# A second pair of heads ahead of the weights, and a new order for the first steps of an attention and two MLPs

## The chip, the cores and the metric

One core of a Trainium2 chip. The time is the device time of one execution in microseconds (us), the median over several runs.

## What is computed

Attention over a causal window of 128 positions with a linear bias per head, then two MLPs one after the other. All of it is float32.

```python
scores = scale * np.matmul(q, k.transpose(0, 1, 3, 2))        # q, k, v: (4, 8, 576, 64)
mask = (rel >= 0) & (rel < 128)
scores = np.where(mask, scores + bias[None], -1000000000.0)
attn = softmax(scores)
x = np.matmul(attn, v) -> (2304, 512)
h = x @ w_in                                                  # (512, 2048)
g = np.where(h >= 1, h, np.where(h <= -1, 0.0, (h + 1) ** 2 / 4))
x = g @ w_out                                                 # (2048, 512)
h = x @ w_in2
out = (h * np.clip(h + 3.0, 0.0, 6.0) / 6.0) @ w_out2
```

The weights reach the chip as 64-bit floats and are turned into 32-bit ones there.

## The kernel before

The tokens are cut into twelve **units** of 64 to 256 tokens (three to a batch). A unit has eight heads, and a head one or two **steps** of up to 128 query rows; the first unit has 256 tokens, so 16 steps. `tick` (L601) makes one step of the attention go one stage further for several steps at once:

- `stage_a` (L414) of the newest step: PE multiplies queries by keys (the scores, L411), VectorE adds the bias table and takes the row's bound (L441, here called the row), ScalarE takes the exponential (L445).
- `stage_b` (L454), two ticks later: PE transposes the probabilities (L469, L470), ScalarE copies them to `tt` (L152).
- `stage_c_whole` (L491), three ticks later: PE multiplies by the values into `r` (L506); at the end of a pair of heads VectorE divides by the sum (L518 to L520).
- `stage_d_whole` (L525), four or five ticks later: PE transposes the result (L531), ScalarE and VectorE split it into the two halves of `x` (L152, L159), which the first MLP reads.

The lags stand in `LAG_B, LAG_C, LAG_D` (L34). In `tick` the older steps' stages come first and `stage_a` last. While the first unit runs, `keep_busy` (L121) puts one matmul of zeros before each step's scores; `WARM_UP` pairs of such matmuls stand at the very start (L851). The tile `zeros` that they read is cleared by VectorE (L846), and ScalarE copies one column of it (L849).

Pairs of heads are loaded by `load_whole` (L307) and `load_values` (L319): two key transfers, one query transfer, one value transfer, all issued by SyncE's queue (SP). A pair's key and query tiles and its value tile are used again by later pairs, so a load waits for the steps that read the tile before. SP works its list strictly in the order in which the code is written; eight transfers may be in flight, since the ninth waits for the first to land. The other engines' lists are put in order by a scheduler, which an edge can bind: `behind` (L630) puts what it encloses behind the newest row on VectorE.

A weight block f is two transfers of 512 KB, `w_in` and `w_out` (L182, L186), given out by `Weights.load` (L172). Its conversion goes in three parts. `conv1` (L189) is two passes of ScalarE (L194, L198) and one of GpSimd (L197); `conv2` (L200) is two of VectorE (L205, L212); `conv3` (L214) is a cast of ScalarE (L152) and a subtraction of VectorE (L159). `conv_tick` (L222) does conv2 and conv3 of one block and conv1 of the next. During the first unit it is called four times, in ticks that the loop at L860 picks out:

```python
for t in range(n_pre):                 # n_pre = 20
    att.tick()
    if t % 2 == 0:
        W1.load()
    if t in (n_pre // 2 - 1, n_pre - 6) or t >= n_pre - 2:
        W1.conv_tick()
```

Then the first MLP begins. `Mlp.first` (L648) makes `h` in twelve matmuls per block (L655), `activate` (L680) makes `g` on VectorE (L684, L686), ScalarE (L685, L152) and GpSimd (L159), and `Mlp1.second` (L691) multiplies by `w_out` into `acc` (L697), two blocks of f later. The attention of the later units and the remaining conversions run between these matmuls.

Of the kernel before, what the change touches and what calls it, by code (L numbers as in the profile page):

```python
# [9 lines left out]
F32 = mybir.dt.float32  # L10
# [5 lines left out]
AF = mybir.ActivationFunctionType  # L16
ALU = mybir.AluOpType

P = 128
# [3 lines left out]
EPS = 1e-09  # L23
# [10 lines left out]
LAG_B, LAG_C, LAG_D = 2, 3, 4  # L34
LAG_B_SPLIT, LAG_C_SPLIT = 3, 5
WARM_UP = 6
WHOLE = 4


@with_exitstack  # L40
def tile_window_attention_two_mlps(
# [15 lines left out]
    nc = tc.nc  # L57
    B, H, D, S = qT.shape
# [189 lines left out]
    for j, (t0, n) in enumerate(units):  # L248
        for h in range(H):
            u = Head()  # L250
# [19 lines left out]
    class Attention:  # L270
# [137 lines left out]
        def scores(self, u, ps, qo, ko, nk):  # L408
            parts = [(u.q, u.k)] if u.whole else [(u.qs, u.kh), (u.qs, u.kl)]
            for w, (q, k) in enumerate(parts):  # L410
                nc.tensor.matmul(ps[:, :nk], q[:, qo:qo + P], k[:, ko:ko + nk],  # L411
                                 start=(w == 0), stop=(w == len(parts) - 1))

        def stage_a(self, n, i):  # L414

            u = heads[n]
# [18 lines left out]
            if not u.whole and a >= P:  # L435
# [8 lines left out]
                scalar=3.0e38, op0=ALU.add, op1=ALU.min, accum_out=sm[:, 0:1])  # L444
            nc.scalar.activation(out=pt[:, :nk], in_=pt[:, :nk], func=AF.Exp, bias=sm[:, 0:1],  # L445
                                 scale=-1.0, accum_out=None if u.whole else sm[:, 1:2])
# [44 lines left out]
        def stage_c_whole(self, n, i):  # L491
# [18 lines left out]
            if j == 0 or i < len(u.qbs) - 1:  # L510
# [6 lines left out]
            rec, r, y = rec[:, :nb], r[:, :nb], y[:, :nb]  # L517
            nc.vector.tensor_scalar(out=rec, in0=r[:, :, 0:2 * D + 2:2 * D + 1], scalar1=EPS, scalar2=None, op0=ALU.add)  # L518
            nc.vector.reciprocal(rec, rec)
            nc.vector.tensor_tensor(  # L520
                out=y, in0=r[:, :, 1:2 * D + 1].rearrange("p b (h d) -> p b h d", h=2),
                in1=rec.rearrange("p b (h o) -> p b h o", o=1).to_broadcast([P, nb, 2, D]), op=ALU.mult)
            u.y = y
# [77 lines left out]
        def tick(self):  # L601
            t = self.t
            self.t += 1
            first, whole = unit_steps[0], sum(unit_steps[:WHOLE])
            for lag, span, stage in ((LAG_D, range(first), self.stage_d_whole),
                                     (LAG_D + 1, range(first, whole), self.stage_d_whole),
                                     (LAG_C, range(whole), self.stage_c_whole),
                                     (LAG_C_SPLIT, range(whole, len(steps)), self.stage_c),
                                     (LAG_B, range(whole), self.stage_b),
                                     (LAG_B_SPLIT, range(whole, len(steps)), self.stage_b)):  # L610
                if t - lag in span:
                    stage(*steps[t - lag])
            if t < len(steps):
                n, i = steps[t]
                u = heads[n]
                self.more_loads(n + 3)
                self.more_preps(n)
                self.stage_a(n, i)
                late, self.late = self.late, []
# [6 lines left out]
            else:  # L626
                while self.late:
                    self.to_x(*self.late.pop(0))

        def behind(self):  # L630
# [206 lines left out]
    with ExitStack() as actx:  # L837
# [10 lines left out]

        nc.scalar.copy(zeros[:, 0:1], nc.const_aps.tensor(0.0, [P, 1], F32))  # L849
        bank = psum.tile([P, BANK], F32, tag="h1", name="busy")  # L850
# [3 lines left out]
        for vt in att.vts:  # L854
            nc.gpsimd.memset(vt[:, :, 0:2 * D + 2:2 * D + 1], 1.0)
        att.more_loads(1)
        W1.load()

        n_pre = unit_steps[0] + LAG_D
        for t in range(n_pre):  # L860
            att.tick()
            if t % 2 == 0:
                W1.load()
            if t in (n_pre // 2 - 1, n_pre - 6) or t >= n_pre - 2:
                W1.conv_tick()

# [469 lines left out]
```

## Time and profile before

| | us |
|---|---|
| median of 3 runs | 948.12 |
| lowest and highest run | 947.30, 948.22 |
| the profiled execution | 946.91 |
| its span, first to last instruction | 945.20 |
| PE busy in the span | 928.9 (98%) |
| VectorE, ScalarE, GpSimd busy | 659.8, 535.4, 306.1 |
| granted clock of TensorE, mean | 0.999 |

The profile is of one execution. Its engines are PE (matmuls; PEld is the loading of weights beside them), DVE (VectorE), ACT (ScalarE), POOL (GpSimd) and SP (SyncE, whose queue is SPq). An operation is named by its line, and out<-in by the tiles it writes and reads. Times in a timeline count from the start of the span.

### The profile page before, as it was taken

Reading aid. Unit: us, or ns where it says so; the run is one execution under the profiler, and the core shown is the slowest. Engines: PE = TensorE matmul, PEld = TensorE weight load, DVE = VectorE, ACT = ScalarE, POOL = GpSimd, SP = SyncE. Lnnn points to the kernel's source line nnn. Section 1 sums busy time; section 2 is a strip of 40 time slices with the busy share of each in tenths; the row PEclk is TensorE's granted clock in tenths of the full one; section 3 lists DMA queues with packets and bytes.
Section 4 is the critical chain, followed back from the end, with each engine's and each line's share of the span. In section 5 each row is a group of like instructions: output and inputs, shape, how many; then the busy total and the mean of one; then the engine's idle time right before and its main releaser. Section 6 shows DMA issues by size and latency. Waiting matters only on the chain.

```text
span 945.2 us, 17238 instructions
## 1 busy us (share of the span) xinstructions
PE 928.9 (98%) x5683; PEld 875.2 (93%) x5683; DVE 659.8 (70%) x1750; ACT 535.4 (57%) x1349; POOL 306.1 (32%) x575
## 2 busy tenths in 40 slices
PE   8899999999999999999999999999999999999998
PEld 6799999999999999999999999999999898888987
DVE  6998975786677677767647989848557777644443
ACT  6998854676667566666636876425333334423233
POOL 3243844787668676777710000000000000000000
PEclk9999999999999999999999999999999999999999
DMA  8858332232222212322007880004264644543441
GB/s 258 238 170 271 107 93 88 68 86 68 73 61 76 77 47 62 88 76 61 3 34 251 298 276 22 1 23 167 79 211 167 235 171 151 169 123 112 122 113 67
DMA packets 95337, 114.90 MB, mean 122 GB/s; under 512 B 8848, under 2 KB 73616, under 8 KB 95248
## 3 DMA queue, kind: packets, MB, share of 16 engines
q1 hardware_dynamic: 95248, 113.80, 38.2%
q8 instruction: 45, 0.74, 0.3%
q14 instruction: 44, 0.36, 0.1%
HBM read 88.60 MB, written 25.17 MB: 120 GB/s over the span
## 4 chain that ended last, share of the span: by engine, by line
PE 85%; DVE 6%; DMA 3%; ACT 3%; issue 1%; POOL 1%; SPq 0%; ACTq 0%; POOLq 0%; DVEq 0%
PE h L655 25%; PE acc L756 21%; PE acc L697 17%; PE y L1237 7%; PE x L1237 5%; PE s L411 3%; PE r L554 3%; DMA rawa<-w_out 2%; PE t L470 2%; PE r L506 1%; DMA rawa<-w_in 1%; DVE kl L391 1%; DVE r L684 1%; DVE r L686 1%; DMA qw<-qT 1%
## 5 line engine op out<-in xcount | busy, mean ns | idle before, releaser
L655 PE MATMUL h<-x,wa 128*128 128x384 f32 (+1 forms) x1344 | 231.0, 317 | 1.2 <-DVE r L686 0.8
L697 PE MATMUL acc<-g,wa 128*128 128x384 f32 (+1 forms) x1344 | 227.7, 315 | 0.4 <-POOL g L159 0.4
L756 PE MATMUL acc<-wb,g 128*128 128x512 f32 x861 | 222.2, 393 | 0.0
L655 PEld LDWEIGHTS h<-x,wa 128*128 128x128 f32 x1344 | 206.6, 189 | 4.3 <-DVE r L686 3.1
L697 PEld LDWEIGHTS acc<-g,wa 128*128 128x128 f32 x1344 | 206.2, 189 | 1.0 <-POOL g L159 0.6
L756 PEld LDWEIGHTS acc<-wb,g 128*128 128x128 f32 x861 | 159.4, 188 | 24.9
L152 ACT CAST g<-r 128x384 fp32r<-128x384 f32 (+1 forms) x208 | 101.3, 487 | 70.4 <-DVE r L1184 37.6
L159 POOL TENSOR_TENSOR g<-r,g 128x256 fp32r<-128x256 f32 (+1 forms) x96 | 93.4, 973 | 67.5 <-ACT g L152 51.4
L685 ACT ACTIVATE r<-r 128x384 f32<-128x384 f32 (+1 forms) x112 | 53.5, 478 | 80.4 <-DVE r L684 79.8
L159 DVE TENSOR_TENSOR g<-r,g 128x384 fp32r<-128x384 f32 x112 | 62.4, 557 | 43.2 <-ACT g L152 42.8
L684 DVE TENSOR_SCALAR r<-h 128x384 f32<-128x384 f32 (+1 forms) x112 | 55.4, 495 | 45.0 <-PE h L655 38.2
L488 POOL TENSOR_SCALAR_AFFINE_SELECT tt<-dist 128x256 fp32r<-128x256 f32 (+1 forms) x176 | 76.5, 455 | 14.0 <-DVE dist L483 13.9
L686 DVE TENSOR_TENSOR r<-h,r 128x384 f32<-128x384 f32 (+1 forms) x112 | 55.8, 499 | 27.9 <-ACT r L685 26.1
L655 PE MATMUL h<-x,wb 128*128 128x384 f32 x384 | 72.5, 336 | 0.0
L655 PEld LDWEIGHTS h<-x,wb 128*128 128x128 f32 x384 | 68.2, 188 | 2.6
L445 ACT ACTIVATE p<-p,sm 128x128 f32<-128x128 f32 (+2 forms) x134 | 57.0, 427 | 21.0 <-DVE sm L441 20.8
L1182 ACT ACTIVATE r<-u 128x384 f32<-128x384 f32 x32 | 16.8, 526 | 56.5 <-DVE u L1246 56.5
L554 PEld LDWEIGHTS r<-tt,vs 128*128 128x128 f32 x304 | 44.7, 189 | 3.1 <-issue 1.4
L393 POOL TENSOR_TENSOR qs<-qr,qs 128x256 fp32r<-128x256 f32 (+2 forms) x64 | 39.4, 616 | 25.1 <-ACT qs L390 13.3
L554 PE MATMUL r<-tt,vs 128*128 128x128 f32 (+3 forms) x304 | 44.3, 262 | 1.3 <-POOL tt L488 0.9
L470 PE MATMUL t<-ident,p 128*128 128x128 f32 x134 | 38.4, 288 | 1.0 <-DVE sm L448 0.5
L391 DVE SCALAR_TENSOR_TENSOR kl<-kr,kh 128x256 fp32r<-128x256 f32 (+3 forms) x64 | 38.9, 608 | 0.0
(161 smaller groups left out, 1553.6 us busy)
## 6 DMA issues: line engine op xcount, KB each, us to landing
w<-wd SPq DMA_DIRECT2D x88, 256.0 KB, 2.7
rawa<-w_in SPq DMA_DIRECT2D x16, 512.0 KB, 5.2
rawa<-w_out SPq DMA_DIRECT2D x16, 512.0 KB, 5.4
rawb<-w_in SPq DMA_DIRECT2D x16, 512.0 KB, 3.9
rawb<-w_out SPq DMA_DIRECT2D x16, 512.0 KB, 4.9
wd<-sum SPq DMA_DIRECT2D x32, 256.0 KB, 2.2
wd<-wb SPq DMA_DIRECT2D x24, 256.0 KB, 2.8
out<-o SPq DMA_DIRECT2D x17, 256.0 KB, 2.2
```

The source lines that it names most:

```text
L152: nc.scalar.copy(hi, x)
L159: engines[eng].tensor_tensor(out=lo, in0=x, in1=hi.bitcast(F32), op=ALU.subtract)
L445: nc.scalar.activation(out=pt[:, :nk], in_=pt[:, :nk], func=AF.Exp, bias=sm[:, 0:1], scale=-1.0, accum_out=None if u.whole else sm[:, 1:2])
L470: nc.tensor.transpose(ps[:, 1, :], pt[:, P:] if u.whole and has_prev else pt[:, :P], ident)
L488: nc.gpsimd.affine_select(out=u.tt[:, :, s0 + s, :m], in_=both, compare_op=ALU.is_ge, fill=0.0, base=-1 + s, pattern=[[0, 2], [sign, m]], ...
L554: nc.tensor.matmul(u.r[:, qo:qo + nq], u.vs[:, j, c, :, :].rearrange("p a d -> p (a d)"), u.tt[:, part].rearrange("p s q -> p (s q)")[:, s ...
L655: nc.tensor.matmul(ps[:, :n], self.W.w_in(a, c, f), self.x_chunk(x, b, c, n), start=(k == 0), stop=(k == 3 * KC - 1))
L684: nc.vector.tensor_scalar(out=r[:, :n], in0=ps[:, :n], scalar1=-1.0, scalar2=1.0, op0=ALU.max, op1=ALU.min)
L686: nc.vector.tensor_tensor(out=r[:, :n], in0=ps[:, :n], in1=r[:, :n], op=ALU.max)
L697: nc.tensor.matmul(acc[i][:, o * n:(o + 1) * n], self.W.w_out(a, f)[:, e * P:(e + 1) * P], g[:, b, :n], start=(first and k == 0 and o == 0 ...
L756: nc.tensor.matmul(acc[t][:, :DM], g[:, b, tg * P:(tg + 1) * P], self.W.w_out(a, f), start=(first and k == 0), stop=(last and k == 2))
L1237: nc.tensor.matmul(ps[:, :N2], w[:, a, c * P:(c + 1) * P], self.x.operand(k, c, b), start=(start and n == 0), stop=(n == 5), skip_group_ch ...
```

## The change

Four things are changed, all in the first unit of the attention:

- Before the loop two pairs of heads are loaded in place of one, and then two weight transfers in place of one; the loop's first tick no longer issues a weight transfer.
- In `tick`, a step of the first unit has its `stage_a` before the older steps' stages. In ticks 4 to 7 the stages c and d are bound behind the newest scores on PE, and the first unit's division is bound behind the newest row on VectorE.
- ScalarE's first copy writes `minus_odd`, which VectorE writes again later, in place of a column of `zeros`.
- The four conversion ticks are 8, 12, 16 and 19 in place of 9, 14, 18 and 19, and what they put on VectorE and ScalarE is bound behind the newest row and the newest exponential.

```diff
+CONV_AT = 8, 12, 16, 19
...
-                nc.tensor.matmul(ps[:, :nk], q[:, qo:qo + P], k[:, ko:ko + nk],
-                                 start=(w == 0), stop=(w == len(parts) - 1))
+                self.score = nc.tensor.matmul(ps[:, :nk], q[:, qo:qo + P], k[:, ko:ko + nk],
+                                              start=(w == 0), stop=(w == len(parts) - 1))
...
-            nc.scalar.activation(out=pt[:, :nk], in_=pt[:, :nk], func=AF.Exp, bias=sm[:, 0:1],
+            self.exp = nc.scalar.activation(out=pt[:, :nk], in_=pt[:, :nk], func=AF.Exp, bias=sm[:, 0:1],
...
+            with self.behind() if u.unit == 0 else ExitStack():
...
+            if t < first:
+                self.more_loads(steps[t][0] + 3)
+                self.more_preps(steps[t][0])
+                self.stage_a(*steps[t])
...
-                    stage(*steps[t - lag])
+                    with self.behind_score(t, lag):
+                        stage(*steps[t - lag])
...
-                self.more_loads(n + 3)
-                self.more_preps(n)
-                self.stage_a(n, i)
+                if t >= first:
+                    self.more_loads(n + 3)
+                    self.more_preps(n)
+                    self.stage_a(n, i)
...
+        def behind_score(self, t, lag):
+            second = range(4, 8)
+            return tc.issue_after(self.score.ins) if t in second and lag > LAG_B else ExitStack()
+
+        def behind_exp(self):
+            return tc.issue_after(self.exp.ins)
...
-        nc.scalar.copy(zeros[:, 0:1], nc.const_aps.tensor(0.0, [P, 1], F32))
+        nc.scalar.copy(minus_odd, nc.const_aps.tensor(0.0, [P, 1], F32))
...
-        att.more_loads(1)
+        att.more_loads(3)
+        W1.load()
         W1.load()
...
-            if t % 2 == 0:
+            if t % 2 == 0 and t > 0:
                 W1.load()
-            if t in (n_pre // 2 - 1, n_pre - 6) or t >= n_pre - 2:
-                W1.conv_tick()
+            if t in CONV_AT:
+                with att.behind(), att.behind_exp():
+                    W1.conv_tick()
```

SP's list, from its fifth transfer on; `kw`, `qw` and `vr` are keys, queries and values of a pair of heads, `rawa` a weight block. Before, then now:

```order
L182 DMA rawa_169<-w_in 128x4x256
L315 DMA kw_106<-kT 64x256
L317 DMA qw_107<-qT 128x256
L315 DMA kw_106<-kT 64x256
L327 DMA vr_103<-v 128x2x128
L186 DMA rawa_169<-w_out 128x1024
L315 DMA kw_kh_109<-kT 64x256
```

```order
L316 DMA kw_106<-kT 64x256
L318 DMA qw_107<-qT 128x256
L316 DMA kw_106<-kT 64x256
L328 DMA vr_103<-v 128x2x128
L183 DMA rawa_173<-w_in 128x4x256
L187 DMA rawa_173<-w_out 128x1024
L316 DMA kw_kh_109<-kT 64x256
```

The second pair's four transfers have moved up past `w_in`; from `w_out` on the list is as it was.

PE's list where the second pair's scores stand (`s` from `kw_106`); `t` are transposes of the probabilities, `r` products with the values of the first pair. Before, from the fourth step's scores on, then now:

```order
L506 MATMUL r_204<-vr_102,tt_188 128x65 x2
L470 MATMUL t_0_219<-ident,p_115 128x128
L469 MATMUL t_1_230<-ident,p_113 128x128
L470 MATMUL t_1_230<-ident,p_113 128x128
L506 MATMUL r_204<-vr_102,tt_218 128x65 x3
L411 MATMUL s_0_222<-kw_106,qw_107 128x128
L411 MATMUL s_1_234<-kw_106,qw_107 128x256
L411 MATMUL s_0_255<-kw_106,qw_107 128x128
```

```order
L412 MATMUL s_0_216<-kw_106,qw_107 128x128
L126 LDWEIGHTS zeros
L126 MATMUL s_1_229<-zeros 128x256
L507 MATMUL r_210<-vr_102,tt_198 128x65 x2
L471 MATMUL t_0_225<-ident,p_115 128x128
L412 MATMUL s_1_229<-kw_106,qw_107 128x256
L507 MATMUL r_210<-vr_102,tt_224 128x65
L470 MATMUL t_1_236<-ident,p_113 128x128
```

The second pair's first scores stood behind all products of the first pair; now they stand ahead of most of them.

VectorE's list where the first conversion step stands (L205 before, L206 now); the ISA instructions are the rows, `p_113` from `s_0_354` before and from `s_0_348` now the first of pair four. Before, then now:

```order
L441 ISA p_113,sm_1_301<-s_1_298,dist 128x256
L441 ISA sm_1_301 128x1
L518 TENSOR_SCALAR rec_310<-r_268 128x4
L205 SCALAR_TENSOR_TENSOR ma_304<-ma_304,rawa_169 128x1024
L519 RECIPROCAL rec_310<-rec_310 128x4
L441 ISA p_114,sm_0_326<-s_0_323,dist 128x128
```

```order
L442 ISA p_115,sm_1_334<-s_1_331,dist 128x256
L442 ISA sm_1_334 128x1
L521 RECIPROCAL rec_316<-rec_316 128x4
L522 TENSOR_TENSOR y_317<-r_274,rec_316 128x256
L442 ISA p_113,sm_0_351<-s_0_348,dist 128x128
L442 ISA sm_0_351 128x1
L206 SCALAR_TENSOR_TENSOR ma_293<-ma_293,rawa_173 128x1024
```

The step has moved back by three rows of the attention.

## Rows read from the trace of the kernel before

**Rows 1.** Busy time by stretch: length; each engine's us and instructions; granted clock; DMA share; GB/s.

```profile
0.00:5.00 5.00, 2.66 (x13) 1.91 (x14) 3.10 (x9) 1.48 (x2) 4.05 (x19) 1.00 0.34 93
5.00:10.00 5.00, 4.78 (x34) 3.79 (x33) 1.72 (x11) 2.80 (x8) 0.93 (x3) 1.00 0.96 296
10.00:15.00 5.00, 4.66 (x33) 3.52 (x32) 2.68 (x14) 3.60 (x10) 0.14 (x1) 1.00 1.04 308
15.00:20.00 5.00, 4.29 (x30) 3.17 (x30) 4.22 (x12) 4.25 (x11) 0.99 (x1) 1.00 1.05 301
20.00:40.00 20.00, 16.01 (x110) 13.46 (x109) 17.69 (x41) 18.43 (x33) 6.85 (x7) 1.00 1.01 291
40.00:60.00 20.00, 19.36 (x148) 18.11 (x148) 19.32 (x48) 18.83 (x40) 6.88 (x8) 1.00 0.38 118
60.00:945.20 885.20, 877.14 (x5327) 831.28 (x5326) 611.07 (x1618) 485.99 (x1249) 286.29 (x540) 1.00 0.36 115
```

The engines stand in the order PE, PEld, DVE, ACT, POOL.

**Rows 2.** Timeline from the start to the first row: start, us, instruction, idle before and releaser.

```profile
0.90 0.17 DVE L846 MEMSET zeros<- 128x128 uint32 x1 [0.90 <-PEq L1329]
...
2.34 2.74 PE L125 MATMUL busy<-zeros 128*128 128x256 bf16 x12 [2.34 <-ACT zeros L849]
...
4.88 0.42 PE L125 MATMUL s<-zeros 128*128 128x256 bf16 x1
...
5.15 0.15 DVE L130 TENSOR_SCALAR minus_odd<-odd 128x1 f32<-128x1 int32 x1
...
5.73 0.29 DVE L441 CUSTOM_DVE_ANT_0 p<-s,dist 128x128 f32<-128x128 f32 x1 [0.43 <-PE s L411]
```

**Rows 3.** Timeline of SP's queue: transfers of pair two, three and four.

```profile
3.79 0.52 SPq L315 DMA_DIRECT2D kw<-kT  x1
...
7.15 0.58 SPq L317 DMA_DIRECT2D qw<-qT  x1
...
11.60 0.35 SPq L317 DMA_DIRECT2D qw<-qT  x1
```

**Rows 4.** Timeline of ScalarE: pair two's exponentials, first conversion, cast of block three.

```profile
11.31 1.15 ACT L445 ACTIVATE p<-p,sm 128x128 f32<-128x128 f32 x3 [1.82 <-DVE sm L441]
...
13.62 1.15 ACT L194 ACTIVATE ma<-rawa 128x1024 f32<-128x1024 f32 x1
...
32.54 1.08 ACT L152 CAST wa<-ma 128x1024 fp32r<-128x1024 f32 x1
```

**Rows 5.** Landing of the query transfers issued at 7.15 and 11.60 us.

```profile
DMA to landing us min/median/max: 5.0/5.0/5.0
...
DMA to landing us min/median/max: 5.5/5.5/5.5
```

**Rows 6.** The transfers' queue in 2:4.5, 4.5:6.6, 6.6:30: packets, MB, mean rate or share.

```profile
DMA packets 553, 0.39 MB, mean 155 GB/s; under 512 B 57, under 2 KB 553, under 8 KB 553
...
q1 hardware_dynamic: 553, 0.39, 55.8%
...
q1 hardware_dynamic: 580, 0.56, 85.5%
...
DMA packets 6067, 7.06 MB, mean 302 GB/s; under 512 B 474, under 2 KB 5434, under 8 KB 6065
```

**Rows 7.** Timeline of PE: pair three's first scores, the first MLP matmul, second products.

```profile
13.73 0.39 PE L411 MATMUL s<-kw_kh,qw 128*128 128x128 f32 x2
...
23.10 0.98 PE L655 MATMUL h<-x,wa 128*128 128x256 f32 x6
...
40.74 0.74 PE L697 MATMUL acc<-g,wa 128*128 128x256 f32 x4 [0.39 <-POOL g L159]
```

**Rows 8.** Timeline of VectorE: first step of the first conversion, and its subtraction.

```profile
16.07 1.25 DVE L205 SCALAR_TENSOR_TENSOR ma<-ma,rawa 128x1024 uint32<-128x1024 uint32 x1
...
21.82 1.23 DVE L159 TENSOR_TENSOR wa<-ma,wa 128x1024 fp32r<-128x1024 f32 x1 [0.22 <-ACT p L445]
```

**Rows 9.** The page's groups: GpSimd's part of g.

```profile
L159 POOL TENSOR_TENSOR g<-r,g 128x256 fp32r<-128x256 f32 (+1 forms) x96 | 93.4, 973 | 67.5 <-ACT g L152 51.4
```

More of the change, by code (lines that the diff above doesn't have):

```diff
@@ L517, in stage_c_whole @@
             rec, r, y = rec[:, :nb], r[:, :nb], y[:, :nb]
[L518 to L522, printed above, removed]
+            with self.behind() if u.unit == 0 else ExitStack():
+                nc.vector.tensor_scalar(out=rec, in0=r[:, :, 0:2 * D + 2:2 * D + 1], scalar1=EPS, scalar2=None, op0=ALU.add)
+                nc.vector.reciprocal(rec, rec)
+                nc.vector.tensor_tensor(
+                    out=y, in0=r[:, :, 1:2 * D + 1].rearrange("p b (h d) -> p b h d", h=2),
+                    in1=rec.rearrange("p b (h o) -> p b h o", o=1).to_broadcast([P, nb, 2, D]), op=ALU.mult)
             u.y = y
```

## The prediction

> **What bounds the kernel now.** I read the table of stretches first, then the page's costliest groups, then the timeline of the first 41 us engine by engine, and last the DMA queue. The table [rows 1] shows TensorE (PE) busy for 877.14 of the 885.20 us after 60 us: from there it sets the pace, and nothing that the diff touches runs there. Before, it is not so. Between 5 and 40 us PE is idle for 0.22 + 0.34 + 0.71 + 3.99 = 5.26 us, between 40 and 60 us for 0.64 us. In the same stretches ScalarE (ACT) works 4.25 of 5 us and 18.43 of 20 us, VectorE (DVE) 4.22 of 5 and 17.69 of 20, and the DMA engines stand at a share of 1.0. So the ramp is where time can be won, it has three limits that lie close together, and the prize is no more than 5.26 + 0.64 us and what the first matmul can move.
>
> A microsecond saved in the ramp is worth a microsecond at the end if PE still has it when its waits are over. The printed order makes that simple to ask: behind the first ninth of PE's list, somewhere before 100 us, both kernels list the same instructions on every engine. The whole difference is how much earlier PE comes to that place.
>
> **The zeros.** Now PE's first weight load waits until 2.34 us for ACT's copy of one column of zeros; VectorE's own write of them ended at 0.90 + 0.17 = 1.07 us [rows 2]. With that copy aimed at another tile, PE starts 1.27 us earlier, and twelve warm-up matmuls and the first filler at (4.88 - 2.34)/12 = 0.21 us each are over at 3.8 us. The first scores follow there, and no longer at 5.1 us. The row behind them does not gain that much: VectorE is writing zeros into key tiles and two small constants until 5.30 us, in both kernels, so the first row moves from 5.73 to 5.30 us, **0.43 us**. The write of the constant now also waits for ACT's copy, which is over before 2.34 us and 2.8 us ahead of it; it costs nothing.
>
> **Pair two ahead of the weights.** SP gives out one transfer in 0.5 us [rows 3]. Four more of them in front of the first weight piece put that piece back by four issues, 2.1 us, and give PE the second pair's queries and keys before 7 us. Now ACT stands idle for 1.82 us before the exponentials of that pair at 11.31 [rows 4]. With the data there and the scores listed ahead of the lagging values, the idle goes, and ACT is through with both pairs near 12 us. It then has nothing, because pair three sits in the queue where it sat. Its queries land at 7.15 + 5.0 = 12.1 us now [rows 3, 5].
>
> They will land later. While only the attention's small transfers are in flight (2 to 4.5 us) the engines' share is 55.8%; in the 2.1 us after that, with the first weight piece among them, 85.5%; from 10 us on it is full, 1.04 and more [rows 1, 6]. In the new order the middle stretch looks like the first one. That loses (0.855 - 0.558) x 2.1 = 0.62 us of work, 0.6 us of every landing behind it while the engines stay full. The bounds: nothing, if the engines catch up because later pieces overlap better, and 1.0 us, if the stretch moves only the 155 GB/s of the first where it could move the 302 of the third: 2.1 x (1 - 155/302). I take 0.6, since it is nearest to what the stretch itself shows. The Trainium skill, "DMA: Bandwidth & Descriptors", section "Measured (HBM→SBUF, 128 partitions, SWDGE, issued from GpSimd)", speaks against this part: it gives 138 GB/s for transfers of 64 KB and 341 for 1 MB, which would make the lag 2.1 x (1 - 138/341) = 1.25 us, an estimate from that page, and the sum below 946.5 us in place of 945.9; the trace agrees in kind, 155 against 302 GB/s, and by less.
>
> So pair three's queries land near 12.7 us, its first exponential stands at 12.7 + 0.3 (second key tile) + 0.4 (scores, [rows 7]) = 13.4 to 13.5 us, and the first conversion behind it at **13.8 us** instead of 13.62 [rows 4]. By then one exponential and one copy more are done, 0.5 us. Net 0.3 us ahead: the idle is not removed, most of it moved from before pair two to before pair three.
>
> **Conversions queued.** This part takes something away. VectorE's first conversion step runs at 16.07 us now [rows 8]. In the new list it stands behind the first row of pair four, whose queries land at 11.60 + 5.5 = 17.1 us [rows 3, 5], 17.7 with the lag. Scores 0.4 and the row 0.3 us bring the step to 18.4 us, **2.3 us later**. Then 1.25, a row of 0.5, 1.25, ACT's cast of 1.08 and the subtraction of 1.23 [rows 4, 8]: the first MLP matmul can start at 23.7 us instead of 23.10 [rows 7], 0.6 us later. In exchange ACT's first conversion runs in one piece, and its second starts right behind pair four's first exponential, at 18.8 us.
>
> I follow ACT's list from there with the durations of these rows (each next instruction starts about 0.1 us before the end of the last). The cast of the first block ends at 22.5 us; then the remaining exponentials and copies of the unit and conversion three bring the second cast to 29.1, and the third begins at 33.8 us, 1.2 us later than the 32.54 of now [rows 4]. But ahead of it in the new list stand five instructions that stand behind it now: an exponential, a copy, a cast of x, one conversion step and a square, 0.4 + 0.3 + 0.3 + 1.07 + 0.3 = 2.3 us. ACT is ahead by 2.3 - 1.2 = **1.1 us**. VectorE, by the same count at its fourth subtraction, is ahead by 0.7 us. Both have 1.57 and 2.31 us of idle between 20 and 40 us now [rows 1], and my count allows for hardly any; that is its weak side.
>
> PE comes out better. The first g needs the third cast, two conversion steps and a cast, 34.7 + 2.1 + 0.3, and POOL's 0.97 us [rows 9]: second products can begin at 38.1 us instead of 40.74 [rows 7], 2.6 us earlier. Whether PE keeps that depends on ACT and DVE, which between 40 and 60 us work 18.83 and 19.32 of 20 us: PE would wait for them again until only their lead is left. I take the engine that I could follow best, ACT with 1.1 us, rounded down to **1.0 us** for the 0.7 of VectorE.
>
> **Sum.** The profiled execution took 946.91 us, 945.20 of it span; less 1.0 us this is 945.9 us. The median of the runs is 1.2 us above that execution, so I forecast 948.12 - 1.0 = **947.1 us**. A measurement of this kernel can tell about 0.2% from no change, 1.9 us, so this counts as no change.
>
> **The rivals.** *PE keeps its lead* (0.27): the waits of the ramp close for good, as VectorE's idle of 2.31 us between 20 and 40 us gives it room to follow. For it: after 60 us PE is all but gapless, so whatever it has then stays. Against it: 19.32 of 20 us on DVE. The end moves by 2.6 us: 945.5 us.
>
> *Nothing is won* (0.12): the lag of 0.6 us goes through, waits of ACT and DVE stay as many as they are, and the first MLP matmul's 0.6 us is never given back. For it: the DMA share is full until 40 us, so landings pace the conversions. Against it: between 40 and 60 us the share is 0.38, so the stream does not set the pace for long. 948.1 to 948.7 us.
>
> *VectorE becomes the bound* (0.06): its first conversion step slips by 2.3 us behind the row of pair four, nothing else is ready for it in that gap, and with 0.68 us of idle between 40 and 60 us it cannot make it up, so PE's second products wait for it. It decides if over 1.9 of the 2.3 us remain at 40 us: 950.4 us, slower. Against it: DVE has 2.31 us of idle before 40 us.
>
> *The clock falls* (0.03): the granted clock is 1.00, the 2.4 GHz level, in every stretch of the table, while fillers still step by 0.21 us before 4.88 us, which is 256 columns at 1.2 GHz. In the new order PE waits near 12 us for pair three with its fillers already issued. If the clock fell there and came back as late after as it rose at first (2.34 to about 5.2 us), 2.9 us would run at half pace: 1.5 us on the forecast, 948.6 us. That TensorE drops to the lower level when it goes idle is what the Trainium skill says in "TensorE: Matmul & The Clock Gate", section "HAM oscillation — how this bites in real kernels"; no row here shows it.
>
> That the change does not do what it says is unlikely; the printed orders show every part in place.
>
> **How the numbers follow.** The forecast case has 0.52, and its own range is 946.3 to 948.0 us, from the bounds of the lag (0 and 1.0 us in place of 0.6) and 0.3 us on either side for the two leads, 0.7 and 1.1 us. Faster by over 0.2% is the first rival and a little of the forecast's lower end: 0.28. Slower by over 0.2% is VectorE's case alone: 0.06. The rest, 0.66, is no change. The range 945.3 to 948.7 us takes in the first two rivals and leaves out VectorE's case and the tail of the first, less than 2 in 10.
>
> **What the profile of the changed kernel would show.** Right: the first warm-up matmul near 1.1 us, the first row near 5.3, the second pair's exponentials done by 12 us, an idle ACT until about 13.5, the first VectorE conversion step near 18.4, the first MLP matmul at 23 to 24, second products before 39 us, and PE idle of 4 to 4.5 us between 5 and 40. Wrong: pair three landing at 12.1 us or earlier (no lag), DVE idle of over 3 us between 15 and 40, PE idle below 3 us or above 5.5 us there, a granted clock below 1.00 between 11 and 17, or a difference that arises after 100 us.

## The result and the profile after

| | us |
|---|---|
| the kernel before, median of 6 runs | 948.06 (947.30 to 948.52) |
| the changed kernel, median of 6 runs | 954.93 (954.19 to 955.44) |
| ratio, with its 95% interval | 1.0076 (1.0065 to 1.0087) |
| profiled execution and span of the changed kernel | 955.15, 953.4 |

The forecast was 947.1 us and no change; the kernel became 6.9 us slower. The span grew by 8.2 us, 945.2 to 953.4, in the two executions that were profiled.

The table of stretches of the changed kernel, columns as in [rows 1]:

```profile
5.00:10.00 5.00, 4.00 (x26) 2.57 (x25) 2.07 (x14) 2.73 (x8) 0.93 (x3) 1.00 0.83 258
10.00:15.00 5.00, 4.66 (x38) 4.07 (x37) 2.70 (x14) 3.38 (x10) 0.00 (x0) 1.00 1.09 330
15.00:20.00 5.00, 3.17 (x22) 2.28 (x20) 1.72 (x10) 4.11 (x9) 1.11 (x1) 1.00 1.09 311
20.00:40.00 20.00, 15.86 (x99) 13.04 (x97) 16.16 (x36) 15.88 (x30) 5.70 (x5) 0.91 0.87 262
40.00:60.00 20.00, 17.65 (x116) 16.68 (x117) 17.59 (x35) 16.63 (x32) 7.92 (x6) 0.83 0.39 123
```

Read it beside [rows 1]. PE is idle for 7.31 us between 5 and 40 us, where 5.26 us stood. Between 40 and 60 us PE got through 116 matmul instructions where it had got through 148, and it was busy 17.65 us in place of 19.36. From 20 to 40 us VectorE and ScalarE are idle for 3.84 and 4.12 us, where 2.31 and 1.57 stood. And the granted clock, 1.00 everywhere before, is 0.91 and 0.83. Cut where the clock changed, the same view shows two stretches at the 1.2 GHz level, 3.4 and 6.8 us long:

```profile
20.00:24.50 4.50, 2.54 (x20) 1.89 (x18) 4.29 (x9) 4.48 (x8) 2.37 (x3) 1.00 1.12 321
24.50:28.00 3.50, 3.50 (x15) 3.31 (x16) 2.07 (x7) 1.44 (x5) 0.00 (x0) 0.51 0.64 169
28.00:41.50 13.50, 9.83 (x67) 7.84 (x65) 11.29 (x23) 11.46 (x19) 3.67 (x3) 1.00 0.78 245
41.50:48.40 6.90, 6.17 (x27) 5.99 (x28) 5.95 (x13) 4.80 (x9) 4.08 (x3) 0.51 0.25 77
```

Ahead of each PE had waited much: 1.96 of 4.50 us, and 3.67 of 13.50, over half of it just before 41.5, where the clock fell in the midst of a wait. The timelines of PE, VectorE and ScalarE show what for:

```profile
14.70 1.13 ACT L195 ACTIVATE ma<-rawa 128x1024 f32<-128x1024 f32 x1
15.74 1.11 ACT L199 ACTIVATE rawa<-rawa 128x1024 int32<-128x1024 uint32 x1
16.72 0.52 ACT L446 ACTIVATE p<-p,sm 128x256 f32<-128x256 f32 x1
...
17.29 0.33 PE L470 MATMUL t<-ident,p 128*128 128x128 f32 x1 [1.40 <-ACT p L446]
...
23.24 0.44 PE L470 MATMUL t<-ident,p 128*128 128x128 f32 x2 [1.41 <-ACT p L446]
...
36.90 0.42 DVE L701 TENSOR_SCALAR r<-h 128x256 f32<-128x256 f32 x1
37.23 1.22 DVE L213 CUSTOM_DVE_ANT_0 ma<-rawa,ma 128x2048 uint16<-128x2048 uint16 x1
...
39.48 1.23 DVE L206 SCALAR_TENSOR_TENSOR ma<-ma,rawa 128x1024 uint32<-128x1024 uint32 x1 [0.68 <-POOL rawa L198]
40.62 1.22 DVE L160 TENSOR_TENSOR wa<-ma,wa 128x1024 fp32r<-128x1024 f32 x1
41.75 0.42 DVE L703 TENSOR_TENSOR r<-h,r 128x256 f32<-128x256 f32 x1
...
42.23 2.50 PE L672 MATMUL h<-x,wa 128*128 128x256 f32 x10 [2.67 <-DVE r L703]
```

Twice both passes of a conversion (L195, L199) stand on ScalarE ahead of an exponential that PE's transposes need, the second time with one cast of x between them: 1.40 and 1.41 us. Then the scheduler has put two more conversion steps (L206, L160), the first of which waits for GpSimd as well, between the two VectorE instructions that read the first block of h (L701, L703); before, L212 alone stood there, as L213 does here. The third block of h needs the bank (a piece of the memory that PE writes to) that these two free: 2.67 us. The milestones of the prediction, with the rows that answer to [rows 2, 4, 7, 8]:

```profile
1.12 2.74 PE L126 MATMUL busy<-zeros 128*128 128x256 bf16 x12 [1.12 <-DVE zeros L863]
...
5.36 0.29 DVE L442 CUSTOM_DVE_ANT_0 p<-s,dist 128x128 f32<-128x128 f32 x1
...
18.25 0.16 DVE L520 TENSOR_SCALAR rec<-r 128x4 f32<-128x4 f32 x1 [2.68 <-PE r L507]
...
19.90 1.22 DVE L206 SCALAR_TENSOR_TENSOR ma<-ma,rawa 128x1024 uint32<-128x1024 uint32 x1
...
25.62 0.78 PE L672 MATMUL h<-x,wa 128*128 128x256 f32 x2
...
38.99 1.03 ACT L153 CAST wa<-ma 128x1024 fp32r<-128x1024 f32 x1
...
46.98 1.87 PE L714 MATMUL acc<-g,wa 128*128 128x256 f32 x9
```

### The profile page after: what moved, and what is told of

Same layout as the page of the kernel before. It is cut to its first block, busy times and chain, and to the rows that moved or that the text cites. A ratio compares the mean times of both kernels' runs of the same rounds, so it can differ in the third digit from the quotient of the medians.

```text
span 953.4 us, 17243 instructions
## 1 busy us (share of the span) xinstructions
PE 933.6 (98%) x5683; PEld 878.9 (92%) x5683; DVE 661.9 (69%) x1750; ACT 536.1 (56%) x1349; POOL 309.1 (32%) x575
## 4 chain that ended last, share of the span: by engine, by line
PE 86%; DVE 4%; issue 3%; ACT 3%; POOL 2%; DMA 2%; SPq 0%; ACTq 0%; POOLq 0%; DVEq 0%
PE h L672 25%; PE acc L773 21%; PE acc L714 18%; PE y L1256 7%; PE x L1256 5%; PE s L412 3%; PE r L556 3%; PE t L471 2%; PE r L507 1%; DMA rawb<-w_out 1%; DVE kl L392 1%; DVE r L703 1%; DVE r L701 1%; DMA rawa<-w_out 1%; POOL rawa L198 0%
## 5 line engine op out<-in xcount | busy, mean ns | idle before, releaser
L160 POOL TENSOR_TENSOR g<-r,g 128x256 fp32r<-128x256 f32 (+1 forms) x96 | 96.0, 1000 | 73.8 <-ACT g L153 53.3
L160 DVE TENSOR_TENSOR g<-r,g 128x384 fp32r<-128x384 f32 x112 | 62.3, 556 | 43.2 <-ACT g L153 43.0
L701 DVE TENSOR_SCALAR r<-h 128x384 f32<-128x384 f32 (+1 forms) x112 | 55.4, 494 | 45.8 <-PE h L672 38.4
L703 DVE TENSOR_TENSOR r<-h,r 128x384 f32<-128x384 f32 (+1 forms) x112 | 55.8, 498 | 27.4 <-ACT r L702 25.6
L394 POOL TENSOR_TENSOR qs<-qr,qs 128x256 fp32r<-128x256 f32 (+2 forms) x64 | 39.6, 620 | 24.5 <-ACT qs L391 13.0
```

The lines of the kernel that those rows point to most:

```text
L160: engines[eng].tensor_tensor(out=lo, in0=x, in1=hi.bitcast(F32), op=ALU.subtract)
L701: nc.vector.tensor_scalar(out=r[:, :n], in0=ps[:, :n], scalar1=-1.0, scalar2=1.0, op0=ALU.max, op1=ALU.min)
L703: nc.vector.tensor_tensor(out=r[:, :n], in0=ps[:, :n], in1=r[:, :n], op=ALU.max)
```

## The experiments

Each is compared with runs of the kernel before on its own chip, so across chips the ratios are to be compared and not the times. "The 241st" and "the 1001st" matmul are counted without those of zeros; they start at 47.92 and 140.56 us in the first profile of before, and the table says how much later in the run's profile. The clock's column gives where it fell and for how long.

| run | median | ratio, 95% interval | 241st | 1001st | clock at the 1.2 GHz level |
|---|---|---|---|---|---|
| changed kernel | 954.93 | 1.0076 (1.0065 to 1.0087) | +6.79 | +8.15 | 24.5 (3.4), 41.6 (6.8) |
| e1 conversions as before | 951.02 | 1.0040 (1.0026 to 1.0055) | +0.12 | +3.62 | 112.8 (3.4) |
| e2 ticks without bindings | 951.09 | 1.0034 (1.0020 to 1.0048) | +3.56 | +4.70 | 39.0 (6.8) |
| e3 conversions alone | 953.95 | 1.0074 (1.0059 to 1.0089) | +5.72 | +7.18 | 25.8 (6.8), 42.9 (3.4) |
| e4 zeros alone | 952.15 | 1.0050 (1.0032 to 1.0068) | +4.33 | +6.82 | 19.4 (3.4), 39.9 (6.8) |
| e7 loads alone | 954.26 | 1.0074 (1.0059 to 1.0089) | +2.93 | +6.89 | 41.1 (3.4) |
| e8 tick order alone | 949.15 | 1.0011 (1.0001 to 1.0020) | +1.54 | +3.78 | 25.3 (3.4) |
| e10 one warm-up less | 952.60 | 1.0051 (1.0034 to 1.0068) | +4.17 | +6.04 | 28.6 (3.4), 42.2 (3.4) |
| e5 waits filled | 953.12 | 1.0062 (1.0047 to 1.0077) | +4.31 | +7.03 | none |
| e9 maximum ahead | 956.68 | 1.0098 (1.0083 to 1.0113) | +6.07 | +9.35 | 40.6 (6.8) |
| e11 and pass split | 951.75 | 1.0045 (1.0030 to 1.0060) | +3.20 | +4.69 | 38.0 (6.8) |
| e13 and row ahead | 951.31 | 1.0038 (1.0024 to 1.0052) | +2.93 | +4.42 | 38.1 (6.8) |
| e6 zeros, ten warm-ups | 946.38 | 0.9985 (0.9975 to 0.9994) | +0.50 | +0.41 | none |
| e15 the same again | 946.51 | 0.9990 (0.9981 to 0.9999) | +0.66 | +0.33 | none |
| e12 ten warm-ups alone | 947.61 | 1.0005 (0.9996 to 1.0014) | +1.62 | +1.20 | none |
| e14 kernel before | 947.53 | one run | +0.84 | +0.54 | none |

### Which part does it?

The conversions' part undone (e1), its bindings alone undone (e2), then single parts on the kernel before: the conversions (e3), the zeros (e4), the loads (e7), the tick order (e8). The expectations number the parts in the order zeros, loads, tick order, conversions. The edits are those of the diff above; e1 and e2 take out

```diff
-CONV_AT = 8, 12, 16, 19
+CONV_AT = 9, 14, 18, 19
-                with att.behind(), att.behind_exp():
-                    W1.conv_tick()
+                W1.conv_tick()
```

(e2 only the last three lines).

> The changed kernel with its fourth part undone: the conversion ticks are 9, 14, 18, 19 again and nothing binds the conversions; the other three parts stay. Theory Q (the queued conversions do it: ScalarE runs both passes in one piece of 2.1 us ahead of exponentials, TensorE waits 1.4, 1.4 and 2.7 us and its clock falls twice): the granted clock stays at 1.0 after 6 us, and the time is 946.5 to 948.5 us. Rival O (the order of the first steps or of the loads does it): two falls of the clock remain and the time stays within 2 us of 954.9. Rival Z (the early start of the warm-up shifts the clock's falls): a fall near 24 us remains, 951 us or more.

> The changed kernel with the ticks 8, 12, 16, 19 kept but the conversions bound behind nothing, so that the scheduler places them. If the bindings are the cause: no wait of TensorE over 1.2 us between 14 and 24 us, clock 1.0, 947 to 949 us. If the earlier ticks are the cause: waits and falls as in the changed kernel, 953 to 956 us.

> The kernel before with the fourth part alone (ticks 8, 12, 16, 19 and both bindings). Theory Q: waits of 1.4 us for exponentials behind the two passes, at least one fall of the clock, 952 to 956 us. Rival O: 947.5 to 949 us, clock 1.0.

> The kernel before with the zeros alone (ScalarE's copy writes minus_odd). All theories but Z: the first warm-up matmul at 1.1 us, the first row at 5.3 us, and 947.5 to 948.2 us, since pair two's data bound the steps behind it. Rival Z: the clock, up earlier, falls somewhere between 20 and 45 us and the time is 950 us or more.

> The kernel before with the second part alone (two pairs of heads ahead of two weight transfers). The scheduler lays out the lists anew here too. Theory S: what counts is the longest waits of TensorE that the new lists make between 14 and 45 us; 949 to 953 us with a fall of the clock, 947.5 to 949 us without. By the prediction's own working: pair two's exponentials without the idle of 1.82 us, and a gain of up to 1 us: 946 to 947.5 us.

> The kernel before with the third part alone (stage_a ahead of the older stages, stages c and d behind the scores in ticks 4 to 7, the division behind the row). Theory S: 949 to 953 us with a fall of the clock, 947.5 to 949 us without. By the prediction's own working nothing changes while pair two's data come late: 947 to 948 us.

Measured: the bindings matter, since e1 and e2 stand at 1.0040 and 1.0034 against 1.0076; the earlier ticks show in the ramp (+3.56 at the 241st matmul in e2, +0.12 in e1) and not in the time. Alone (e3) the part costs as much as the whole change. But theory Q, which put the loss on it, does not hold: e1 and e2 are above every case that Q gave, and the zeros alone cost 5 us, the loads alone 6.6 us (more than any case had), the tick order 1.5 us by the medians and 1.0 by the ratio. Rival O is out too. Rival Z's case came true in e4, but the sections below show that the start is not what did it. The prediction's own working for the single parts, no change or a gain, is out, for the tick order narrowly. Added up, the four single parts would cost 20 us, three times what the change costs, so it is no sum of parts. In e1 the ramp is clean, +0.12 us at the 241st matmul; the loss stands near 112 us. PE's timeline there, with the clock falling at 112.8 us behind it:

```profile
112.66 2.64 PE L714 MATMUL acc<-g,wa 128*128 128x256 f32 x11 [2.08 <-POOL g L160]
```

### The lists, with no part of the change

A one-number edit of the kernel before, which takes two matmuls of zeros from its very start, makes the scheduler lay out the engines' lists exactly as in e4, but for the copy that e4 changes. By the traces VectorE's list then differs from that of before as far as its 286th instruction (129.3 us) and ScalarE's as far as its 226th (125.5 us).

```diff
-WARM_UP = 6
+WARM_UP = 5
```

> The kernel before with five warm-up pairs in place of six: no part of the change, two matmuls of zeros fewer at the very start. The scheduler then lays out VectorE's and ScalarE's lists as in the run of the zeros alone, instruction for instruction. Theory S: 949.5 to 953.5 us, as that run, with its wait of 1.2 us for y near 18 us and falls of the clock. Rival P (in that run the early start did it): 947 to 948.5 us.

Theory S (what costs is that the scheduler lays out the lists anew and PE gets longer waits by it, and not the edit itself) holds, at 952.60 us here and 952.15 in e4. Timelines of VectorE and PE in this run:

```profile
16.24 1.22 DVE L205 SCALAR_TENSOR_TENSOR ma<-ma,rawa 128x1024 uint32<-128x1024 uint32 x1
...
18.27 1.20 DVE L212 CUSTOM_DVE_ANT_0 ma<-rawa,ma 128x2048 uint16<-128x2048 uint16 x1
19.38 0.42 DVE L520 TENSOR_TENSOR y<-r,rec 128x256 f32<-128x256 f32 x1
...
19.85 0.44 PE L531 MATMUL x<-ident,y 128*128 128x128 f32 x2 [1.15 <-DVE y L520]
...
41.38 0.39 PE L655 MATMUL h<-x,wa 128*128 128x256 f32 x1 [1.20 <-DVE r L686]
```

Before, the first conversion step (L205) stood inside the division, which began at 15.95 us, and PE waited 0.16 us for its product. Now the division begins behind that step, at 17.61 us, and the second step (L212) stands inside it, between the reciprocal and the product (L520): PE waits 1.15 us. At 41 us the maximum (L686) has a step ahead of it, as in the changed kernel.

### The zeros with the lists of before

With ten warm-up pairs in place of six and the zeros of the change, the scheduler leaves the lists of VectorE, ScalarE and PE as they were (e6, e15); e12 has the ten pairs alone.

```diff
-WARM_UP = 6
+WARM_UP = 10
-        nc.scalar.copy(zeros[:, 0:1], nc.const_aps.tensor(0.0, [P, 1], F32))
+        nc.scalar.copy(minus_odd, nc.const_aps.tensor(0.0, [P, 1], F32))
```

> The kernel before with the zeros alone, as in the run of the zeros alone, but ten warm-up pairs in place of six; with these the scheduler leaves every list of VectorE, ScalarE and TensorE as it was before the change. Theory S (the zeros alone cost 5 us because the scheduler lays out the lists anew, and TensorE gets longer waits): 946.5 to 948 us, clock at 1.0, since the lists are those of before. Rival P (an earlier start of TensorE shifts where its clock is judged): the clock falls in some runs and the time is 949.5 us or more.

> The kernel before with ten warm-up pairs and nothing else; all lists stay as they were. The warm-up ends some 0.8 us later than before. If the run of the zeros with ten pairs was faster because TensorE starts 1.2 us earlier: this one is 947.5 to 949 us, 1 us or more above that run. If the longer warm-up itself helped: 946 to 947 us.

> The kernel before, unchanged, for its profile on the chip of these runs. Its lists and clock as in its first profile: time between 946.3 and 948.5 us, clock at 1.0, second products at 40 to 41 us.

> The run of the zeros with ten warm-up pairs again, on the chip of the kernel before's second profile, to see where its gain of 1.3 us arises. If the start gives it: the difference to that profile is there before 15 us and stays. If it is a matter of waits behind 40 us that fall out one way or the other: 0 to 0.5 us later than before up to 40 us, and a ratio between 0.9975 and 1.0005.

The same edit of the zeros that cost 5 us with new lists costs nothing with the old ones; rival P is out. e6 is the one version that beats both kernels: 0.15% below before, and 0.10% when run again, both intervals just below 1. Against e12, which differs by the zeros alone, it stands at 0.9985 where e12 has 1.0005, and its start is 1.22 us earlier (first warm-up at 1.12 against 2.34 us). Where it gains on the kernel before is not settled: the profiled execution of e15 was its slowest (947.58 us); it is only 0.2 us ahead of e14 from 14 to 141 us, and the two spans are the same, 945.8 us. It starts its first scores later; PE's timelines of e15, then of e14:

```profile
1.12 4.45 PE L125 MATMUL busy<-zeros 128*128 128x256 bf16 x20 [1.12 <-DVE zeros L846]
...
5.57 0.64 PE L411 MATMUL s<-kw,qw 128*128 128x128 f32 x2
...
14.44 0.39 PE L411 MATMUL s<-kw_kh,qw 128*128 128x128 f32 x2
```

```profile
5.09 0.64 PE L411 MATMUL s<-kw,qw 128*128 128x128 f32 x2
...
14.63 0.39 PE L411 MATMUL s<-kw_kh,qw 128*128 128x128 f32 x2
```

The kernel before varies here by itself: pair three's scores stand at 13.73 us in its first profile [rows 7] and at 14.63 in e14, the second products at 40.74 and at 41.59, later than the 40 to 41 us expected. The clock rose at 5.3 us in the one and 7.3 in the other, and the two spans are 945.2 and 945.8 us. A longer warm-up that costs no start would leave less work at half pace; that is a reading, not shown.

### The clock against the waits

Here matmuls of zeros stand where PE waits in the changed kernel; `fill` puts them into a bank that is free there.

```diff
+FILL = {(4, 1): 10, (6, 1): 12}
+FILL_H = 16
...
+            if (n, i) == (10, 1):                    # in stage_a, behind the scores
+                with tc.issue_after(self.score.ins):
+                    fill("acc0", FILL_H)
...
+            if (n, i) in FILL:                       # in stage_b, ahead of the transposes
+                with tc.issue_after(self.score.ins):
+                    fill("h1", FILL[n, i])
```

> The changed kernel, with matmuls of zeros put on TensorE where it waits: 10 ahead of the transposes at 17.3 us, 12 ahead of those at 23.2 us, 16 ahead of the third block's h at 42.2 us. At 0.107 us each they fit into the waits of 1.40, 1.41 and 2.67 us; the other instructions keep their places on TensorE, VectorE and ScalarE but for two rows. Theory C (the waits let the clock fall, and the half pace costs most of the loss): no fall before 60 us, and 949.0 to 951.0 us, that is 954.9 less the 5.1 us that 10.24 us at half pace cost. Rival W (the waits themselves, or work that they delay, are the loss, and the clock costs little since PE waits anyway): the clock may stay up, but 953 to 955.5 us.

The clock stayed up, and 1.3 us came back, 1.0062 against 1.0076, not the 5.1 us that theory C asked for; the two intervals overlap, so this is no more than an estimate. (The lists moved by a little more than expected: a write of 0.80 us on VectorE at 22.85 us stands behind 110 us in e5.) PE's timeline:

```profile
17.34 0.33 PE L483 MATMUL t<-ident,p 128*128 128x128 f32 x1 [0.33 <-ACT p L456]
...
41.12 1.46 PE L685 MATMUL h<-x,wa 128*128 128x256 f32 x10 [0.96 <-DVE r L716]
...
47.27 0.70 PE L419 MATMUL s<-kw,qw 128*128 128x256 f32 x2 [1.50 <-DVE sm L452]
```

PE comes to what it waits for at the same time (17.34 against 17.29 us) or 1.1 us earlier (41.12 against 42.23), and then waits for the next row. From PE's first scores to its 1001st matmul the stretches of before, the changed kernel and e5 are, columns as in [rows 1]:

```profile
5.09:140.56 135.47, 129.12 (x1016) 121.37 (x1016) 114.55 (x300) 112.12 (x246) 61.17 (x75) 1.00 0.64 195
3.90:148.71 144.81, 133.77 (x1017) 125.14 (x1017) 117.38 (x303) 113.71 (x246) 65.46 (x78) 0.96 0.60 184
3.90:147.59 143.69, 135.08 (x1054) 125.40 (x1054) 117.96 (x303) 114.28 (x246) 66.68 (x78) 1.00 0.60 185
```

By busy time alone half of the 9.3 us that the changed kernel loses here would be the clock's: PE is idle for 4.69 us more and busy for 4.65 us more. In e5 the clock did not fall. Idle time and matmuls of zeros (by the same view 3.96, 3.93 and 8.56 us) come to 10.3 us before, 15.0 in the changed kernel and 17.2 in e5: with the clock up PE is faster at its work and waits longer for the same inputs. Rival W holds for the changed kernel: the waits are the loss, the clock a small part on top.

### Taking the waits away

In e9 the conversion of the fourth block on VectorE is bound behind the first block's maximum; e11 has that, and the second pass of the first two conversions one tick later, so that an exponential stands between the passes; in e13 VectorE's next row passes the fourth block's first step too.

```diff
+                with tc.issue_after(mlp1.max.ins) if W1.n_conv == 4 else ExitStack():    # e9
                     while W1.n_conv < ... and W1.conv_tick():
...
+SPLIT = 8, 12                                                                            # e11
...
+                W1.split = t in SPLIT
...
+            if t - 1 in SPLIT:
+                with att.behind_exp():
+                    W1.conv1b(W1.n_conv - 1)
...
+                if W1.n_conv == 4 and conv0 == 4 and not after:                          # e13, with att.behind()
+                    att.tick()                                                           # in the line of e9
```

> The changed kernel with one binding more: the conversion of the fourth block on VectorE stands behind the first block's maximum, which frees the bank of h. Up to there all lists stay; the maximum passes two steps of 1.22 us, one of which waited 0.68 us for GpSimd. Theory S: TensorE's wait of 2.67 us for the third block's h goes to under 1 us, the second fall of the clock with it, and the time is 950 to 952.5 us. If the first two waits and the first fall set the loss: 954 to 955.5 us.

> The run with the maximum ahead, and in it the second pass of the first two conversions one tick later, behind the next exponential, so that an exponential stands between the two passes on ScalarE. Theory S: the waits of 1.40 and 1.41 us at 17 and 23 us go to under 0.8 us each, no fall of the clock before 45 us, and 947 to 950 us. If what is lost is lost behind 45 us: no change against the run with the maximum ahead.

> The run with the maximum ahead and the pass split, and in it the row of the eleventh pair's... of step 21 ahead of the fourth block's first conversion step on VectorE: one swap, all lists else as in that run but for TensorE's order among a few rows between 45 and 50 us. In that run this step took 2.16 us and TensorE waited 3.00 us for the row behind it. If waits that are taken away come back: the row is 2 us earlier and the time 948.5 to 950 us. If the wait moves on to the next late thing, the first block's g, which GpSimd finishes at 38.9 us: TensorE waits there instead, and the time is 951 to 952 us, as without the swap.

e9 missed: 956.68 us. The wait for h went, and PE's next instructions were the second products, for which g was not made. Timelines of PE and GpSimd in e9:

```profile
40.36 0.59 PE L714 MATMUL acc<-g,wa 128*128 128x256 f32 x2 [1.87 <-ACT g L153]
...
43.47 0.58 PE L714 MATMUL acc<-g,wa 128*128 128x256 f32 x1 [2.52 <-POOL g L160]
```

```profile
40.09 1.65 POOL L198 TENSOR_SCALAR rawa<-rawa 128x1024 f32<-128x1024 f32 x1 [1.70 <-ACT ma L195]
41.71 1.70 POOL L160 TENSOR_TENSOR g<-r,g 128x256 fp32r<-128x256 f32 x1
```

A pass of a later block's conversion stands ahead of g on GpSimd. e11 took the wait of 1.40 us to 0.39 and left none of the second that PE's timeline shows, and at the 161st matmul (35.64 us before) its PE was 1.36 us **ahead** of the kernel before. It lost 4 us by the 201st (42.78 us before), the clock fell at 38 us, and the time stayed above the case that theory S gave. Timelines of VectorE, GpSimd and PE in e11:

```profile
32.59 1.22 DVE L214 SCALAR_TENSOR_TENSOR ma<-ma,rawa 128x1024 uint32<-128x1024 uint32 x1
...
36.14 2.16 DVE L214 SCALAR_TENSOR_TENSOR ma<-ma,rawa 128x1024 uint32<-128x1024 uint32 x1
...
36.11 1.11 POOL L199 TENSOR_SCALAR rawa<-rawa 128x1024 f32<-128x1024 f32 x1 [1.31 <-ACT ma L196]
...
38.69 1.22 PE L420 MATMUL s<-kw,qw 128*128 128x256 f32 x2 [3.00 <-DVE sm L450]
```

With that row ahead of the step of 2.16 us (e13), two waits stand in PE's timeline in place of the one:

```profile
36.63 0.70 PE L420 MATMUL s<-kw,qw 128*128 128x256 f32 x2 [0.96 <-DVE sm L450]
...
38.95 0.58 PE L722 MATMUL acc<-g,wa 128*128 128x256 f32 x1 [1.05 <-POOL g L161]
```

3.00 us became 0.96 and 1.05, and 951.75 us became 951.31, no difference clear of noise: the wait moved on, as the second case said.

## Why the prediction was wrong, point by point

- **The zeros** came as worked out: first warm-up at 1.12 us (1.1 forecast), first row at 5.36 (5.30). That a later list would be laid out anew by it was in the printed orders; that this costs 5 us by itself (e4, e10) was not seen.
- **Pair two ahead of the weights**: its exponentials lost their idle of 1.82 us, and the last of them began at 12.19 us. The lag of 0.6 us hardly arose: pair three's queries landed 5.1 us after an issue at 7.14 us, 12.3 us against the 12.7 forecast and 12.1 before. By the estimate from the Trainium skill's figures ("DMA: Bandwidth & Descriptors", section "Measured (HBM→SBUF, 128 partitions, SWDGE, issued from GpSimd)") the lag would have been 1.25 us; the trace, with 0.2 us, does not agree.
- **Conversions queued** is where the working failed, and first in what VectorE's first step waits for. It was priced by a landing: pair four's queries at 17.7 us, the step at 18.4. They landed 4.9 us after an issue at 11.85 us, at 16.7, sooner than forecast, and the step still came at 19.90, 3.8 us later than before and not 2.3. Behind ScalarE's two passes (14.70 us, 13.8 forecast) an exponential began at 16.72 us whose row VectorE had done at 15.0; so PE's transposes were late, so the copies, the values and the next rows, all back on the same two engines. VectorE's 2.68 us of idle ahead of 18.25 us came from PE's values. The first MLP matmul stood at 25.62 us (23.7), the third cast at 38.99 (33.8) and the second products at 46.98 (38.1). The step that failed is "I follow ACT's list from there with the durations of these rows", with a count that "allows for hardly any" idle. ScalarE and VectorE did not run through their lists: they had 4.12 and 3.84 us of idle between 20 and 40 us. "ACT is ahead by 1.1 us" became, by the same count, 4.1 us behind: the third cast came 5.2 us after the 33.8 worked out.
- **"PE comes out better"** failed with it. The prediction followed the lists of ScalarE and VectorE and did not ask, for each instruction of PE, when its input is made. The two instructions L701 and L703 with conversion steps between them stood in the printed lists.
- **"Behind the first ninth ... both kernels list the same"** is not so, and it was taken to mean that nothing more is lost there. In the trace of before, the last instruction that stands elsewhere in the changed kernel's lists is at 107.6 us on PE, 120.4 on GpSimd, 125.0 on VectorE and 127.9 on ScalarE. Another 1.4 us was lost between the 241st and the 1001st matmul (+6.79 to +8.15), most of it behind 100 us, which the prediction had named as a sign of being wrong. PE's and GpSimd's timelines of the changed kernel show the place, with g behind `vs` on GpSimd:

```profile
117.45 3.12 POOL L160 TENSOR_TENSOR vs<-vr,vs 128x192 fp32r<-128x192 f32 x2
120.54 1.70 POOL L160 TENSOR_TENSOR g<-r,g 128x256 fp32r<-128x256 f32 x1
...
122.30 1.57 PE L714 MATMUL acc<-g,wa 128*128 128x256 f32 x11 [1.31 <-POOL g L160]
```

- **The rivals.** "VectorE becomes the bound" (0.06, 950.4 us) had the right sign, and its first condition came true: the step slipped, nothing was ready in the gap, and PE waited for VectorE ahead of the second products. But VectorE was not too full to catch up, as the rival had it: it was idle for 2.41 us between 40 and 60 us, where 0.68 stood. The price of 2.3 us was too small, since it counted the slip once and not the waits that follow from it. "The clock falls" (0.03) came true in kind, at 24.5 and 41.6 us and not near 12 us, where the clock was 1.00. The rule cited there (the Trainium skill, "TensorE: Matmul & The Clock Gate", section "HAM oscillation — how this bites in real kernels") agrees with the rows in that the level fell behind waits; here no wait between the first rise and the first fall was longer than 1.41 us, and e5 puts what the two falls cost at some 1.3 us of 6.9.
- **The chances.** A 0.28 for faster rested on the prize of 5.26 us of idle. e11 shows that a part of it could be had for a while, PE 1.36 us ahead of the 35.64 us of before; the lists behind gave it back. A loss of 6.9 us was in no case, and the nearest had 0.06.

Between the 241st and the 1001st matmul PE lost 2.5 us in e4 and 4.0 in e7 as well, and their PE timelines show waits at much the same place as in the changed kernel and in e1, and in e7 one more at 81 us:

```profile
123.76 0.41 PE L507 MATMUL r<-vr,tt 128*128 128x65 f32 x2 [1.46 <-ACT g L153]
```

```profile
81.20 0.66 PE L506 MATMUL r<-vr,tt 128*128 128x65 f32 x4 [1.47 <-ACT tt L152]
...
120.31 1.57 PE L697 MATMUL acc<-g,wa 128*128 128x256 f32 x11 [1.31 <-POOL g L159]
```

The first line is of e4, the others of e7. Between 104 and 122 us the kernel before has no wait longer than 0.41 us.

What remains open: e13 is still 3.6 us above the kernel before. The waits that are left, 1.05 us for g and those behind 100 us, were not taken away one by one, so that the waits make up the whole of the loss is read from the traces and from e5, and not shown by a version with the edits and without the loss.

## What to carry to other kernels

Where a scheduler sets the lists, compare a change with a control that only makes the scheduler lay them out anew: here two matmuls of zeros fewer cost as much as a real edit, and the same edit of the zeros with the old lists was free. Where two or three engines near their limit feed each other in a ring, go through the bottleneck engine's list and ask of each instruction where its input stands in the other lists; an engine's own list followed alone gives a time that it cannot keep. Moving one short step ahead of the long ones need not pay: in e9 the wait for a bank went and the time rose, and only with the exponentials moved as well (e11) did it fall, by 4.9 us and not to that of before. Look for what the bottleneck would wait for next before moving the thing that it waits for now.

## What the hardware showed beyond that

VectorE and GpSimd slow each other when both work on weights, and the one that begins second pays: the same step of VectorE took 1.22 us where it began ahead of GpSimd's pass (e11, 32.59 against 33.14 us) and 2.16 us where it began 0.03 us behind the start of a pass of 1.11 us (36.14 us), and GpSimd's part of g, 0.97 us in the mean before [rows 9], took 1.70 us beside VectorE (e9, 41.71 us). This agrees with what the Trainium skill says in "SBUF — State Buffer", section "🎯 Summary: rules for kernel authors": with two inputs in SBUF on VectorE, while GpSimd reads SBUF, the second of the two to issue is held until the first is done. The 0.94 us that the step grew by are near the whole of the other's 1.11 us.

Executions of one kernel differ in when the clock first rises, 5.3 and 7.3 us in two profiles of the kernel before, and where PE's waits are long also in whether it falls: among the four runs of e4 the mean granted clock was 0.994, 0.994, 0.996 and 0.999, and the times 953.78, 952.69, 951.61 and 949.51 us. Whether the falls cost that in e4, or waits that fall out longer in one run than in another cause both, is not shown; in the changed kernel the three executions at 0.994 took 954.60 us in the median and the three at 0.996 took 954.99.
